# Two frequency classes per row in the intermediate matrix, and half of three constant matrices loaded instead of whole

## The chip, the cores and the metric

The kernel runs on one core of a Trainium2 chip. The metric is the time of one execution on the device in microseconds (us); lower is better. TensorE multiplies matrices from SBUF into the eight banks of PSUM; VectorE and ScalarE move results from PSUM to SBUF and do the elementwise work; GpSimd (POOL in the profile) clears tiles and issues DMAs; SyncE (SP) issues DMAs. All tiles have 128 partitions.

## What is computed

For `x` of 8 batches x 5696 positions x 128 channels and a filter `h` of 5696 x 128:

```
Xf = rfft(x, n=2*S, axis=1);  Hf = rfft(h, n=2*S, axis=0)
y  = irfft(Xf * Hf, n=2*S, axis=1)[:, :S, :]        # long convolution, per channel
X  = rfft(y, axis=1)                                # S = 5696
Y[:, :64] = X[:, :64] mixed by the complex 128x128 matrices w_r[m] + i*w_i[m]; the other modes are 0
u   = y + irfft(Y, n=S, axis=1)
out = u + relu(u @ w_ch)
```

Inputs and output are float32. The kernel computes in float16 with float32 sums.

## The kernel before, in words

**Names.** S = 5696 = 64 x 89 positions. J = 64, NQ = 89. The frequencies of the long transform fall into NK = 90 classes k of 64 each. The batches are worked on in four pairs (g_ = 0 to 3). NT = 23 ticks of four classes (the last has two) make up a pair's pass.

**Forward stages.** The first stage transforms over the 89 rows (`a_tile`, tile As), the second, per class, over the 64 (`tick`, tile M). In `products` the spectrum is multiplied by the filter's spectrum Hs into U, on VectorE. In two of three ticks ScalarE first casts the spectrum out of PSUM into Xs, and VectorE reads two SBUF tiles; in the others it reads PSUM.

**Z.** Two ticks later TensorE multiplies U by the constants Wc, and ScalarE casts the result into a buffer Zs or Zt: 128 rows (real and imaginary part of 64 positions p), and per class 256 numbers (two batches x 128 channels). SyncE stores each tick's Z to the DRAM scratch `zscr`, with a DMA row of 256 numbers (512 B) for each class and row. One tick later Z is also multiplied by the constants G. That sums the 64 low modes of y into PSUM bank 7, from which they go to XT.

**Mode products.** After the last pair 128 matmuls with 16 columns each multiply XT by the weights W (loaded during the last pair's ticks), giving Y. Eight transposes by the identity Id turn Y into C.

**Last stage.** `u_z` makes y from Z, `u_c` adds the 64 modes, and both sum in the same PSUM banks, four pairs of banks in turn (`LSLOT`). `u_tile` casts a half tile (eight positions p x 89, one batch) into UT, on ScalarE or VectorE by a fixed pattern whose first cast is VectorE's. `o_tile` multiplies UT by w_ch and the identity (tile WI), and ScalarE and VectorE make the output rows, which SyncE stores.
Z comes back in 16 chunks (four per pair, each 16 positions p of all classes). Row (k, real or imaginary) is the contracted index, 180 rows in all: the first 128 in the tile ZT`i`a with the constants S4a, and the other 52 in partitions 32 to 83 of ZT`i`b with the constants S4b (84 partitions used, of which the first 32 are cleared by GpSimd). So each position p takes two matmuls of 89 columns. The modes take one matmul with the constants IB (tile IBs) per four positions. S4a, S4b and IB have 5696 columns, in the order p, q.

**Five chunk buffers.** There are NC = 5 pairs of ZT tiles. They lie over space that the earlier stages have used: chunks 0 and 2 over Hs, 1 and 3 over As, 4 over M and G. `load_zt` (L469) issues the loads. Chunks 0 to 4 are issued by GpSimd, and per chunk in this order: first half, clear of 32 partitions (L477), second half. Chunks 5 to 15 are issued by SyncE as soon as the chunk five before has been used.

**What sets the order.** Each engine works through its own list in the order in which the program records it; a recorder adds semaphore waits from the named tokens of reads and writes. GpSimd's list in the last pair is written out in the dictionary `early` (L492), keyed by tick: Id and the four quarters of W, S4b at tick 12, S4a at tick 16, and at tick 21 chunk 0, IB, chunk 1 and chunk 2. Each also waits for the product of its tick (`pace`), and chunk 0 for the stores of Z up to tick 14 (`SLACK`). After the last tick come WI and chunks 3 and 4.
TensorE's list at the change of stage is: filler matmuls, the 128 mode products, `u_z` without the modes for the first two half tiles (`alone`, each bank opened by a matmul on a zeroed strip of F1), the eight transposes, `u_z` for a third half tile, and then the regular half tiles. The casts of Y (L304 on VectorE, L300 on ScalarE) and C (L306, L302) stand between them.
Lines of helpers in the profile: L300, L302 (ScalarE casts, without and with a scale), L304, L306 (the same on VectorE), L309 (every DMA), L312 (every matmul), L528 (the products), L690 (the transposes), L735 and L736 (the output's relu and sum).

Of the kernel before, what the change touches and what calls it, by code (L numbers as in the profile page):

```python
# [4 lines left out]
P = 128  # L5
# [118 lines left out]
def bass_long_conv_fft__then__afno_spectral_mix_kernel(nc, x, h, moe_w_r, moe_w_i, moe_w_ch, out):  # L124
# [3 lines left out]
    J = 64  # L128
# [29 lines left out]
    s4 = np.stack([back[:, None, None] * np.cos(ang), -back[:, None, None] * np.sin(ang)], axis=0)  # L158
    RB, PB = 2 * NK - P, 32
    rows = s4.transpose(1, 0, 2, 3).reshape(2 * NK, S)  # L160
    s4t = np.zeros((P, 2 * S))
    s4t[:, 0:S] = rows[0:P]
    s4t[PB:PB + RB, S:2 * S] = rows[P:2 * NK]
    tt = np.arange(S)
# [22 lines left out]
    c_s4 = const("cS4", s4t)  # L187
    c_ib = const("cIB", ib.reshape(P, -1))
    c_g = const("cG", g)
# [12 lines left out]
    def take(nbytes):  # L202
# [36 lines left out]
    f1_sb = at("F1", 2 * NK, F16, take(2 * NK * 2))  # L239
    wc_sb = at("Wc", 2 * P, F16, take(2 * P * 2))  # L240
    XTW = 3 * M
    xt = at("XT", B * XTW, F16, a_g + GW * 2 + 2048 * (NZX - NZ))
    assert GW * 2 + 2048 * (NZX - NZ) + B * XTW * 2 <= HW * 2

    ZB = 16
    NC = 5
    ZP = ZB * 2 * D
    a_h2, a_xt = a_h + HW * 2, a_x + 4 * S + 2 * B * P
    a_as1, a_m2 = a_as + 2 * S, a_m + 4 * S
    zt_off = [(a_h, a_h2), (a_as1, a_as1 + 2 * ZP), (a_h + 2 * ZP, a_h2 + 2 * ZP), (a_as1 + 4 * ZP, a_as1 + 6 * ZP),  # L250
              (a_m2, a_g)]
    assert 2 * S + 8 * ZP <= AW * 2
    zt = [[at(f"ZT{i}{'ab'[p_]}", ZP, F16, zt_off[i][p_]) for p_ in range(2)] for i in range(NC)]
    ib_sb = at("IBs", S, F16, a_m)
# [4 lines left out]
    u_sb = [at(f"UT{i}", S, F16, u_off[i]) for i in range(4)]  # L259
    o_big = [a_h + 4 * ZP, a_h2 + 4 * ZP, a_st + 4 * S] + [a_g + 2 * ZP + 4096 * i for i in range(2)] + \  # L260
            [a_xt + 4096 * i for i in range(2)]
# [22 lines left out]
    R = Recorder(nc)  # L284
    for name, n in (("c", 16), ("x", 26), ("z", 8), ("w", 16), ("t", 10), ("s", 8), ("o", 12), ("p", 16), ("q", 10)):
        R.ring(name, n)
# [87 lines left out]
    for i in range(MP):  # L374
        lo, hi = i * KP * 3 * J, (i + 1) * KP * 3 * J + (J if i == MP - 1 else 0)
        dma("gpsimd", m_sb[:, lo:hi], bass.AP(c_m, lo, [[MW, P], [1, hi - lo]]), "x", (), [("m", i)])
    dma("sync", wc_sb[:, :], bass.AP(c_w, 0, [[3 * P, P], [1, 2 * P]]), "c", (), [("wc",)])

# [87 lines left out]
    ZX = [("zs", i, b) for i in range(NZ, NZL) for b in range(2)]  # L466
    zt_old = [(H_ALL, H_ALL), (AST, AST), (H_ALL, H_ALL), (AST, AST), (M_ALL[3:6], G_ALL)]

    def load_zt(i, eng="sync", more=()):  # L469
        g_, c_ = divmod(i, J // ZB)  # L470
        for part, (p0, r0, n) in enumerate(((0, 0, P), (PB, P, RB))):
            old = once(("zt", i % NC, part), zt_old[i % NC][part])
            if more:
                old = list(old) + list(more)
            if old and part:
                z32 = zt[i][1][0:PB, :].bitcast(U32)
                R.add("gpsimd", lambda e: e.memset(z32, 0), (), [("zt0", i)], after=old)  # L477
            dma(eng, bass.AP(zt[i % NC][part], p0 * ZP, [[ZP, n], [1, ZP]]),
                bass.AP(zs, (g_ * 2 * NK + r0) * J * 256 + c_ * ZB * 256, [[J * 256, n], [1, ZP]]),
                "q" if eng == "gpsimd" else "t", [("zd", g_, s_) for s_ in range(NT)], [("zt", i % NC, part)], after=old)  # L480

    def load_ib():
        dma("gpsimd", ib_sb[:, :], c_ib.ap(), "p", (), [("ib",)], after=M_ALL[0:2] + pace)

    def load_s4(part):
        n = PB + RB if part else P
        dma("gpsimd", s4_sb[part][0:n, :], bass.AP(c_s4, part * S, [[2 * S, n], [1, S]]), "p", (),
            [("s4", part)], after=pace + (AST if part else M_ALL[1:4]))

# [3 lines left out]
             12: lambda: load_s4(1), 16: lambda: load_s4(0),  # L493
             NT - 2: lambda: (load_zt(0, "gpsimd", SLACK), load_ib(), load_zt(1, "gpsimd"), load_zt(2, "gpsimd"))}
    pace = []
# [41 lines left out]
    def tick(g_, t):  # L537
# [22 lines left out]
        if LC <= t < NT + LC:  # L560
            s_ = t - LC
            n = len(ticks[s_])
            i, zi = s_ % NU, s_ % NZS[g_]
            zb = [turns("z", ZBANK) for b in range(2)]
            for b in range(2):
                for r in range(2):
                    mm(pv(zb[b], 0, [[1, n * D]]), (W1, W2)[r], u_s[i][:, r * 1024 + b * 512:r * 1024 + b * 512 + n * D],
                       r == 0, r == 1, [("u", i), ("wc",)], [bank(zb[b])])
                evac(bass.AP(z_s[zi], b * D, [[1024, P], [2 * D, n], [1, D]]),
                     pv(zb[b], 0, [[D, n], [1, D]]), [bank(zb[b])], [("zs", zi, b)], eng="scalar",  # L570
                     after=once(("zx", zi, b), Z_OLD) if zi >= NZ else ())
            zo = (g_ * NK + KT * s_) * P * 256
            dma("sync", bass.AP(zs, zo, [[256, P], [P * 256, n], [1, 256]]),
                bass.AP(z_s[zi], 0, [[1024, P], [256, n], [1, 256]]), "z",
                [("zs", zi, 0), ("zs", zi, 1)], [("zd", g_, s_)])
# [45 lines left out]


    load_wi()
    load_zt(3, "gpsimd")
    load_zt(4, "gpsimd")

# [5 lines left out]
    def u_z(i, b, half, alone=False):  # L632
# [3 lines left out]
        for hb in range(2):  # L636
# [5 lines left out]
            for pl in range(4):  # L642
                for ri in range(2):
                    pz = half * 8 + hb * 4 + pl
                    so = (c_ * ZB + pz) * NQ
                    n = (P, PB + RB)[ri]
                    mm(pv(t + hb, pl * NQ, [[1, NQ]]), z[ri][0:n, pz * 256 + b * P:pz * 256 + b * P + P], s4_sb[ri][0:n, so:so + NQ],
                       False, not alone and pl == 3 and ri == 1, [("zt", i % NC, ri), ("zt0", i % NC), ("s4", ri)], [bank(t + hb)])
        if alone:
# [3 lines left out]
    def u_c(i, b, half, t, hb, first_):  # L653
# [3 lines left out]
           ib_sb[:, (c_ * ZB + pl0) * NQ:(c_ * ZB + pl0 + 4) * NQ], first_, not first_,  # L657
           [("c", g_ // 2), ("ib",)], [bank(t + hb)])

# [15 lines left out]

    XTT = [(n, g_) for g_ in range(NP) for n in ("xt", "xtn")]
    keep(10, 4)
    for m in range(M):
# [5 lines left out]
    for hb in range(2):  # L684
        evac(bass.AP(y_sb, hb * 32 * B, [[2 * M * B, P], [B, 32], [M * B, 2], [1, B]]),
             pv(hb, 0, [[2 * B, 32], [B, 2], [1, B]]), [bank(hb)], [("y", hb)], eng="scalar" if hb else "vector",
             after=ZY)
# [6 lines left out]
    for hb in range(2):  # L694
        evac(c_sb[:, hb * 512:hb * 512 + 512], ps16[:, (2 + hb) * 1024:(2 + hb) * 1024 + 512], [bank(2 + hb)],
             [("c", hb)], 2.0 * 64 / S, eng="vector" if hb else "scalar", after=WT)


    n_o = [0]
    o_cur = [0]  # L700
    o8_old = [H_ALL] * 2 + [U_ALL] + [G_ALL + ZX] * 2 + [WT] * 2
    o_old = [H_ALL] * 2 + [M_ALL[5:6]]
# [98 lines left out]
```

## Time and profile before

| what | us |
|---|---|
| three timed runs | 404.64, 406.85, 407.57 (median 406.85) |
| the profiled execution, its time | 409.74 |
| its span in the trace | 407.7 |
| TensorE busy | 376.7 (92%) |
| VectorE busy | 311.8 (76%) |
| ScalarE busy | 296.4 (73%) |
| GpSimd busy | 81.4 (20%) |

The DMA queues moved 105.81 MB in 86,720 packets, 72,286 of them under 2 KB. Queue q1 is SyncE's, q0 GpSimd's. In the profile a tile's buffer number is mostly left out, PE is TensorE, PEld its weight loads, DVE VectorE, ACT ScalarE. A line of the wait list reads: engine, tile, line, what it waited for, total us, times, longest. A line of the DMA issues reads: destination, source, queue, count, KB each, median us from issue to landing. Busy time of TensorE counts a matmul from its start to its modelled end, so its shares are read together with the clock.

### The profile page before, as it was taken

To read this page: it belongs to the slowest core of one execution; us is meant where nothing else is said; L and a number is where in the kernel's file an instruction comes from. 1 tells how busy PE (TensorE), PEld (TensorE's weight loads), DVE (VectorE), ACT (ScalarE), POOL (GpSimd) and SP (SyncE) were. 2 spreads that over 40 slices of the span, in tenths; PEclk is the share of its full clock that TensorE was granted. 3 is DMA by queue.
4 is the path that set the end of the run, shared out by engine and by line. 5 is a ranking of instruction groups with operands and counts; after the bars stand their busy time and mean duration, and the time that the engine had idled before them with its cause. 6 is when DMAs were issued, how large, how long until landed. Compare 5 with 4: busy or idle time off the path is not lost.

```text
span 407.7 us, 12527 instructions
## 1 busy us (share of the span) xinstructions
PE 376.7 (92%) x5398; PEld 286.7 (70%) x5398; DVE 311.8 (76%) x341; ACT 296.4 (73%) x477; POOL 81.4 (20%) x133
## 2 busy tenths in 40 slices
PE   7979899998999988899989899997978999999994
PEld 7978666656756657656658666665767889888873
DVE  6878789997899997889997888850324677777876
ACT  1458599987978977788878888960434777777775
POOL 8300022210823202723304011039100000000000
PEclk9999999999999999999999999995798999999999
DMA  8997379995989993989985499999998999999869
GB/s 159 194 320 271 101 162 280 274 278 159 138 137 218 251 233 80 141 154 207 245 224 95 48 311 346 285 274 394 417 390 340 314 350 420 406 419 390 347 251 357
DMA packets 86720, 105.81 MB, mean 260 GB/s; under 512 B 22494, under 2 KB 72286, under 8 KB 82846
## 3 DMA queue, kind: packets, MB, share of 16 engines
q1 hardware_dynamic: 62379, 67.73, 48.1%
q0 software_dynamic: 24288, 37.31, 43.0%
q8 instruction: 42, 0.69, 0.7%
q14 instruction: 11, 0.09, 0.1%
HBM read 72.49 MB, written 51.12 MB: 303 GB/s over the span
## 4 chain that ended last, share of the span: by engine, by line
PE 56%; DMA 14%; DVE 11%; ACT 9%; POOL 6%; issue 2%; SPq 0%; DVEq 0%; POOLq 0%
PE ps L312 56%; DVE U L528 5%; DMA ZT4b<-zscr 5%; DVE As L306 5%; DMA Xr<-in_x_dram 4%; ACT As L302 4%; DMA zscr<-Zt 3%; POOL Xr L309 2%; DMA Hs<-Hs 2%; ACT Xs L300 2%; ACT R L735 1%; ACT UT L300 1%; ACT Zt L300 1%; DVE Xin L348 1%; POOL ZT1b L477 0%
## 5 line engine op out<-in xcount | busy, mean ns | idle before, releaser
L528 DVE TENSOR_TENSOR U<-Xs,Hs 128x2048 f16<-128x2048 f16 x70 | 82.7, 1190 | 20.2 <-ACT Xs L300 20.0
L312 PE MATMUL ps<-U,Wc 128*128 128x512 f16 (+1 forms) x368 | 93.6, 377 | 1.9 <-DVE U L528 1.9
L300 ACT CAST Zs<-ps 128x512 f16<-128x512 f32 (+1 forms) x142 | 75.7, 592 | 9.4 <-PE ps L312 9.4
L300 ACT CAST Xs<-ps 128x1024 f16<-128x1024 f32 x70 | 69.4, 996 | 15.6 <-PE ps L312 14.6
L736 DVE TENSOR_TENSOR O<-ps,R 128x512 f32<-128x512 f32 x81 | 52.5, 685 | 20.4 <-ACT R L735 12.0
L735 ACT ACTIVATE R<-ps 128x512 f32<-128x512 f32 x96 | 50.9, 572 | 18.8 <-PE ps L312 18.4
L306 DVE TENSOR_SCALAR As<-ps 128x720 f16<-128x720 f32 x68 | 57.6, 900 | 9.1 <-PE ps L312 8.5
L312 PE MATMUL ps<-As,M 64*128 64x128 f16 x1440 | 55.8, 217 | 5.1 <-ACT Xs L300 2.0
L312 PE MATMUL ps<-F,Xin 128*128 128x180 f16 x512 | 53.5, 249 | 7.0 <-DVE As L306 2.8
L312 PEld LDWEIGHTS ps<-F,Xin 128*128 128x128 f16 x512 | 44.6, 155 | 14.5 <-DVE As L306 4.1
L302 ACT ACTIVATE As<-ps 128x720 f16<-128x720 f32 x60 | 46.3, 785 | 10.6 <-PE ps L312 9.7
L312 PE MATMUL ps<-WI,UT 128*128 128x256 f16 x360 | 52.3, 280 | 0.5 <-DVE O L736 0.4
L312 PEld LDWEIGHTS ps<-As,M 64*128 64x128 f16 x1440 | 40.7, 94 | 15.1 <-DVE U L528 3.2
L312 PEld LDWEIGHTS ps<-U,Wc 128*128 128x128 f16 x368 | 29.1, 98 | 31.6 <-DVE U L528 2.4
L528 DVE TENSOR_TENSOR U<-ps,Hs 128x2048 f16<-128x2048 f32 x22 | 50.2, 2283 | 0.8 <-DMA Hs<-Hs 0.8
L309 POOL DMA_DIRECT2D Xt<-in_x_dram x48 | 25.5, 536 | 109.7 <-PE ps L312 94.7
L300 ACT CAST UT<-ps 128x712 f16<-128x712 f32 x40 | 30.0, 752 | 20.7 <-PE ps L312 19.7
L312 PEld LDWEIGHTS ps<-WI,UT 128*128 128x128 f16 x360 | 39.4, 152 | 4.3 <-issue 1.9
L312 PE MATMUL ps<-IBs,C 128*128 128x356 f16 x128 | 40.6, 327 | 0.6
L312 PEld LDWEIGHTS ps<-G,Zs 128*128 128x128 f16 x556 | 28.1, 96 | 14.9
L304 DVE CAST UT<-ps 128x712 f16<-128x712 f32 x24 | 21.4, 891 | 17.0 <-PE ps L312 17.0
L312 PE MATMUL ps<-G,Zs 128*128 128x128 f16 (+2 forms) x556 | 34.3, 192 | 0.0
(84 smaller groups left out, 497.0 us busy)
## 6 DMA issues: line engine op xcount, KB each, us to landing
out_dram<-O SPq DMA_DIRECT2D x39, 512.0 KB, 8.3
zscr<-Zs SPq DMA_DIRECT2D x68, 256.0 KB, 6.2
Xt<-in_x_dram POOLq DMA_DIRECT2D x24, 320.0 KB, 6.9
zscr<-Zt SPq DMA_DIRECT2D x20, 256.0 KB, 6.9
W<-wscr POOLq DMA_DIRECT2D x4, 1024.0 KB, 8.5
M<-cM POOLq DMA_DIRECT2D x5, 720.0 KB, 20.4
ZT0a<-zscr SPq DMA_DIRECT2D x3, 1024.0 KB, 9.9
Hs<-Hs SPq DMA_DIRECT2D x44, 64.0 KB, 5.9
```

The lines of the kernel that those rows point to most:

```text
L300: R.add(e, lambda h_: h_.copy(dst, src), reads, writes, after=after)
L302: R.add(e, lambda h_: h_.activation(dst, src, COPY, scale=scale), reads, writes, after=after)
L304: R.add(e, lambda h_: h_.tensor_copy(dst, src), reads, writes, after=after)
L306: R.add(e, lambda h_: h_.tensor_scalar_mul(dst, src, scale), reads, writes, after=after)
L309: R.add(eng, lambda h_: h_.dma_start(dst, src), reads, writes, ring=ring, after=after)
L312: R.add("tensor", lambda h_: h_.matmul(o, l, r, start=st, stop=sp), reads, writes)
L348: R.add("vector", lambda e: e.tensor_copy(bass.AP(x_sb, i * XN * XS, [[XW, NQ], [XS, XN], [1, D]]), bass.AP(src, 0, [[XB, NQ], [D, XN], [1 ...
L528: R.add("vector", lambda e: e.tensor_tensor(uv, src, hv, MULT), bk + [("h", t, 0), ("h", t, 1, 0), ("h", t, 1, J)], [("u", i)])
L735: R.add("scalar", lambda e: e.activation(rv, src_r, RELU), bk, [("r", i % NR)], after=once(("r", i % NR), G_ALL + XTT + [("y", 0), ("y", 1 ...
L736: R.add("vector", lambda e: e.tensor_tensor(ov, src_u, rv, ADD), bk + [("r", i % NR)], [key + (h_,)], after=once(key, old))
```

## The change

**Z by pairs of classes.** `zscr` now holds, per pair of classes (k, k+1) and row p, 512 numbers side by side. A store writes rows of 512 numbers (1 KB), half as many. A chunk's contracted index becomes (pair of classes, real or imaginary), 90 rows of 16 positions x 512 numbers (16 KB). The two matmuls of a position p take the even and the odd class of the same rows.

**Rows spread.** A chunk is one tile ZT`i` of 128 partitions. 64 rows go to partitions 0, 2, ..., 126 and 26 rows to partitions 1, 5, ..., 101. The other 38 partitions must be zero, so GpSimd clears the whole tile (128 x 4096 words of 4 bytes) once, before its first load. The clears of chunks 1 and 0 are recorded at ticks 14 and 17, those of 2, 3 and 4 just before their loads. All chunk loads, 5 to 15 too, are issued by GpSimd.

**Half of the constants.** S4a and S4b (now the constants of the even and the odd classes) and IB are loaded only for the positions p = 0 to 32 (SH = 33 x 89 = 2937 columns). S4a and S4b are cleared by GpSimd first (128 x 2848 words each) and loaded in the same spread rows. The columns of p = 33 to 63 are those of 64 - p, read backwards, with a sign that depends on the row: `reflect` multiplies by a column of the small table SG (128 x 3, loaded by SyncE). VectorE makes the mirrored part of S4a and IB, ScalarE that of S4b. Those of S4 are recorded before the mode products, that of IB after the casts of C. The chunks with p from 32 on wait for them.

**Moved with it.** The two casts of Y change engines (the first bank's to ScalarE, the second's to VectorE). Two of the output buffers move from the space of G to that of M. GpSimd's ring of chunk semaphores grows from 10 to 12.

```diff
+    SH = (J // 2 + 1) * NQ
+    s4t = s4[..., :].transpose(1, 0, 2, 3).reshape(NK // 2, 2, 2, S).transpose(0, 2, 1, 3)[..., 0:SH].reshape(NK, 2 * SH)
+    sg = np.ones((P, 3))
...
-    c_ib = const("cIB", ib.reshape(P, -1))
+    c_ib = const("cIB", ib.reshape(P, -1)[:, 0:SH])
...
+    SPREAD = ((0, J, 0, 2), (J, NK - J, 1, 4))
...
+    zt = [at(f"ZT{i}", 2 * ZP, F16, zt_off[i]) for i in range(NC)]
...
+    zt_old = [H_ALL, AST, H_ALL, AST, G_ALL + ZX + ZY]
+
+    def load_zt(i, more=()):
         g_, c_ = divmod(i, J // ZB)
+        old = list(once(("zt", i % NC), zt_old[i % NC])) + list(more)
+        for part, (r0, n, p0, st) in enumerate(SPREAD):
+            dma("gpsimd", bass.AP(zt[i % NC], p0 * 2 * ZP, [[st * 2 * ZP, n], [1, 2 * ZP]]),
+                bass.AP(zs, g_ * NK * P * 256 + r0 * J * 512 + c_ * ZB * 512, [[J * 512, n], [1, 2 * ZP]]),
+                "q", [("zd", g_, s_) for s_ in range(NT)] + [("zc", i % NC)], [("zt", i % NC, part)], after=old)
+
+    def clear_zt(i):
+        z32 = zt[i][:, :].bitcast(U32)
+        R.add("gpsimd", lambda e: e.memset(z32, 0), (), [("zc", i)], after=list(zt_old[i]) + pace)
...
+    def reflect(eng, t, n, col, key, after):
+        MN = S - SH
+        dst, src = bass.AP(t, SH, [[S, n], [1, MN]]), bass.AP(t, SH - NQ - 1, [[S, n], [-1, MN]])
+        sc = sg_sb[0:n, col:col + 1]
...
+            R.add(eng, lambda e: e.activation(dst, src, COPY, scale=sc), toks, [key + (1,)], after=after)
...
+            R.add(eng, lambda e: e.tensor_scalar_mul(dst, src, sc), toks, [key + (1,)], after=after)
...
+        s32 = s4_sb[part][:, :].bitcast(U32)
+        R.add("gpsimd", lambda e: e.memset(s32, 0), (), [("s4z", part)], after=old)
+        for h_, (r0, n, p0, st) in enumerate(SPREAD):
+            dma("gpsimd", bass.AP(s4_sb[part], p0 * S, [[st * S, n], [1, SH]]), bass.AP(c_s4, (r0 * 2 + part) * SH, [[2 * SH, n], [1, SH]]),
+                "p", [("s4z", part)], [("s4", part, 0, h_)], after=old)
...
              12: lambda: load_s4(1), 16: lambda: load_s4(0),
-             NT - 2: lambda: (load_zt(0, "gpsimd", SLACK), load_ib(), load_zt(1, "gpsimd"), load_zt(2, "gpsimd"))}
+             14: lambda: clear_zt(1),
+             17: lambda: clear_zt(0),
+             NT - 2: lambda: (load_zt(0, SLACK), load_ib(), load_zt(1), clear_zt(2), load_zt(2))}
...
-            dma("sync", bass.AP(zs, zo, [[256, P], [P * 256, n], [1, 256]]),
-                bass.AP(z_s[zi], 0, [[1024, P], [256, n], [1, 256]]), "z",
+            dma("sync", bass.AP(zs, zo, [[512, P], [P * 512, n // 2], [1, 512]]),
+                bass.AP(z_s[zi], 0, [[1024, P], [512, n // 2], [1, 512]]), "z",
...
+    pace[:] = []
     load_wi()
-    load_zt(3, "gpsimd")
-    load_zt(4, "gpsimd")
+    clear_zt(3)
+    load_zt(3)
+    clear_zt(4)
+    load_zt(4)
...
+    reflect("vector", s4_sb[0], P, 0, ("s4", 0), M_ALL[1:4])
+    reflect("scalar", s4_sb[1], P, 1, ("s4", 1), AST)
     keep(10, 4)
...
+    reflect("vector", ib_sb, P, 2, ("ib",), M_ALL[0:2])
```

## The prediction

> **What bounds the kernel now.** I read the page's forty slices first, then the wait list, the chain of waits, the DMA issues, and two-microsecond windows around the gap. The slices:
>
> ```profile
> DVE  6878789997899997889997888850324677777876
> PEclk9999999999999999999999999995798999999999
> DMA  8997379995989993989985499999998999999869
> ```
>
> A slice is 10.2 us. Up to 270 us, and again from 312 us, TensorE is nearly always busy (its share is 99% in the stretch 320 to 340). Between them, in slices 27 to 31, VectorE falls to 0 to 5 tenths, the granted TensorE clock falls to 5 tenths, and only the DMA stays full. The windows there (columns: TensorE, weight loads, VectorE, ScalarE and GpSimd busy time, then granted clock, DMA share, GB/s):
>
> ```profile
> 276.00:278.00 2.00, 1.85 (x51) 1.44 (x47) 0.29 (x1) 0.52 (x1) 2.00 (x3) 0.52 0.91 295
> 278.00:280.00 2.00, 0.23 (x1) 0.10 (x1) 0.00 (x0) 0.07 (x1) 2.00 (x3) 0.50 1.14 409
> 288.00:290.00 2.00, 2.00 (x13) 1.09 (x11) 0.90 (x1) 0.78 (x2) 0.00 (x0) 0.56 1.03 420
> 304.00:306.00 2.00, 0.20 (x1) 0.10 (x1) 0.00 (x0) 0.29 (x1) 0.00 (x0) 1.00 0.99 389
> 308.00:310.00 2.00, 2.00 (x20) 1.65 (x18) 0.90 (x1) 0.56 (x1) 0.00 (x0) 0.50 0.81 336
> ```
>
> TensorE stands still twice, at 278 to 280.8 and 303.6 to 307, and it works at half clock from about 276 to 289.6 and from 306.9 to 310.2. The wait list between 270 and 320 us names the causes:
>
> ```profile
> POOL ZT0a L309 <- DMA zscr<-Zt: 10.0, 1, 10.0
> PE ps L312 <- DMA ZT4b<-zscr: 2.4, 1, 2.4
> PE ps L312 <- DMA ZT0b<-zscr: 2.4, 1, 2.4
> PE ps L312 <- DMA ZT3b<-zscr: 0.7, 1, 0.7
> PE ps L312 <- DMA ZT4a<-zscr: 0.7, 1, 0.7
> ```
>
> All are loads of the Z chunks. The chain of waits says why they are late:
>
> ```profile
> 260.02 10.88 DMA zscr<-Zt
> ...
> 271.95 1.81 POOL ZT0b L477
> 273.76 0.46 POOL ZT0b L309
> ...
> 286.47 20.44 DMA ZT4b<-zscr
> ```
>
> The first Z load waits until a Z store issued at 260.0 has landed at 270.9; then GpSimd clears 32 partitions (1.8 us) between the two halves of each chunk; and the last half of chunk 4, issued at 286.5, needs 20.4 us. Transfers of the same kind took, by the DMA issues (KB each, us to landing):
>
> ```profile
> ZT1a<-zscr POOLq DMA_DIRECT2D x1, 1024.0 KB, 12.0
> S4b<-cS POOLq DMA_DIRECT2D x1, 934.5 KB, 8.5
> ZT0b<-zscr POOLq DMA_DIRECT2D x1, 416.0 KB, 7.1
> ZT4b<-zscr POOLq DMA_DIRECT2D x1, 416.0 KB, 20.4
> ```
>
> The 20.4 us are a queue: from 290.8 on, SyncE issues chunks 5 to 8 (5.9 MB) on its own queue, and they share the DMA with chunks 3 and 4 that GpSimd issued before.
>
> **The change, part by part.** The profiled execution took 409.74 us (span 407.7, 2.0 around it), which is 2.9 above the median 406.85 of the three runs and above all of them. I sum against 409.74 and carry the difference to the median.
>
> *Z stores.* The 46,080 rows of 512 B (4 pairs x 90 classes x 128) become 23,040 of 1 KB. Most transfers of Z are written while TensorE is busy, so this shows only as relief of the DMA. Windows rich in 512 B rows move 268 to 271 GB/s at shares of 0.86 to 0.96 (264 to 268 us); windows of 8 KB reads move 409 to 446. A store of 256 KB therefore costs at most 0.97 us of DMA and at least 0.6; I take 0.77 for the 1 KB rows, between them. Over the last pair's 11 ticks from 250 to 270 us that is 2.2 us of DMA time. Before 250 us the only stalls on transfers are VectorE's, on Hs (0.8 us) and on Xt (1.1 us): gain 0 to 1.9, taken 0.5.
>
> *Constants.* S4a, S4b and IB shrink from 3782 KB to 1767 KB (2 x 90 rows and 128 rows of 5874 B). At 410 GB/s that is 5.0 us of DMA time, 3.3 of them before 270 us. Together with the stores, some 5 us of backlog vanish before 270, so the store that the first load waits for should land near 265. The next gate is the pacing on the last product but one, which VectorE ends at 269.9. So the first Z load starts about 270.0 instead of 271.4.
>
> *GpSimd's new order.* A memset of 32x2048 words took 1.82 us, 0.89 ns a word; 128 partitions should cost no more, as the four 128x1 memsets at the start took 0.10 to 0.11 us each. So a chunk's clear (4096 words) costs 3.65 us and S4's (2848) 2.53. Two of each come before the first load, with four issues of 0.53: from 253.5 (S4b's start in the trace) the chain is S4b to 257.1, chunk 1 to 260.8 (its product, of tick 14, ends at 257.0), S4a from its present gate at 260.9 to 264.5, chunk 0 to 268.1. That leaves 1.8 us until 269.9: no cost, but thin. Then chunk 0 is issued by 271.0 (its second half left at 273.7 before), IB by 271.6, chunk 1 by 272.7, the clear and issues of chunk 2 by 277.4, WI, chunk 3 by 283.2, chunk 4 by 287.9, against 287.0 before. Chunk 4 gets 0.9 us later and is not needed until about 300.
>
> *Chunk 0.* Its landing takes between 3.4 us (1440 KB at 420 GB/s) and 12.0 (chunk 1's row); nearest is ZT0b's own 7.1, with less traffic ahead of it. From 270.6 that gives 277.7. TensorE ends the mode products and the filler matmul at 277.85 and restarted at 280.84: 3.0 us of standstill go. That work is at half clock. If the clock comes back at 289.6 as now, the 3.0 us are worth 1.5; if it comes back one dip (3.3 us, the length of the second one) sooner, 1.65 more; two sooner, 3.3 more. Range 1.5 to 4.8, taken 3.0.
>
> *Chunks 3 and 4.* All loads are now on GpSimd's queue, so chunk 5 comes behind chunk 4. A chunk is 1440 KB, 3.6 us of DMA at 410 GB/s, and TensorE takes 3.93 us for one (SyncE's chunk loads left at 290.80, 294.73, 298.67). Chunk 4 lands by 288 + 7.1 = 295, and is needed at 300. The waits of 0.7, 0.7 and 2.4 us go (3.8), and with them the second dip, 3.3 us at half clock: 1.65. Lower end: half, if the queue is still late (below); upper end 5.45.
>
> *Reflections.* ScalarE's on S4b: 2759 elements at the 996 ns per 1024 of the Xs casts, 2.7 us. VectorE's: between 0.92 us (the Xin copy, 2048 in 0.68) and 3.07 (2048 in 2.28 from PSUM); I take 3.07, as the start is odd and the source runs backwards. The two on S4 run from 273.4 to 276.5. Queued behind them are the Y casts (ready at 275.6 and 277.5) and behind those the transposes, which TensorE reaches at about 282: hidden; if that cover were gone, 3.1 us. IB's waits on VectorE for the C cast, about 283.2, and ends at 286.3. Behind it stands the first UT cast, ready at 285.6, whose bank TensorE wants back two half tiles later. Price 0 to 3.1, taken 0.6.
>
> *Nothing else on the path.* Matmuls keep their number and their 89 columns; 84 rows become 128, and both kinds took 203 ns medians. SyncE loses 22 issues in the last stage (0.3 to 0.9 us each) and GpSimd, idle there, gains them. The later stage needs a chunk every 6.7 us, far slower than they load. The small sign table loads at the start, ahead of Wc, which is not needed before 30 us.
>
> Sum: 0.5 + 3.0 + 3.8 + 1.65 - 0.6 = 8.35 us. 409.74 becomes 401.4, and on the median's scale 406.85 becomes **398.5**. Its own range, from the ends above, is 394.5 to 402.5.
>
> **Rivals.**
>
> *The reflection waits for GpSimd.* IB's reflection and the clear of chunk 4 (283.2 to 286.8) want to start together. If the clear goes first and holds VectorE, the reflection ends at 289.9, the first UT cast at 290.8, and TensorE loses up to 3.6 us less the half tile it has in hand: 401. Against it: the Y cast of 0.69 us ran at 275.6 inside a GpSimd memset at its normal length (O's 685 ns for as many elements); but that read PSUM, and no row has VectorE reading and writing SBUF beside a memset. [...]
>
> *The transfers stay late.* The DMA share is 0.8 to 1.14 in every window from 276 to 310, so a new order makes no bandwidth. If chunk 0 gains nothing and chunk 4 only the 1.7 us of the smaller IB, the second dip stays, and some 2.3 us with the 0.5 above remain: 404.5. Against it: chunks 5 to 8, which competed with 3 and 4, move behind them.
>
> *Slower: the clears under the products.* From 250 to 270 us VectorE is busy for 16.76 of 20 us, and GpSimd has no memset there now. If a clear advances only while VectorE rests (16% of the time), 2.7 of the 12.4 us are done by 269.9; the other 9.7 and the 2.1 of issues put the first load at 281.7 and its landing at 289.3, 8.5 later than now. With 5.45 still won behind it, 0.6 paid and the rest lost to the longer idle clock: 411. It decides from about 1.6 ns a word on: then chunk 0 lands 5 us late and the change is worth nothing. For it: only 1.8 us of slack. Against it: 0.89 ns in all five memsets, but all with VectorE idle or on PSUM.
>
> **How the numbers follow.** Forecast 0.56 (394.5 to 402.5); reflection held 0.08 (401); transfers late 0.20 (404.5); slower 0.16 (411). About 1%, 4.1 us, is what a measurement can tell from no change: below 402.8 is faster, above 410.9 slower. Faster: 0.56 + 0.07 + 0.03 = 0.66. Same: 0.01 + 0.17 + 0.03 = 0.21. Slower: 0.13. The range 394.5 to 405.0 leaves out the slower rival and the tails.
>
> **What would show it.** Right: memsets of 128x4096 at 3.6 us and none ending after 270; chunk 0 issued near 270; no wait of TensorE on any ZT load; no second clock dip; the reflections at 0.9 to 3.1 us with the first UT cast no later than 288. Wrong: a ZT4 wait of microseconds (transfers), memsets over 5 us before 270 (slower), or a reflection that begins just as a memset ends (held). What would make the number wrong with the mechanism right is mainly where the clock returns.

## The result, and the profile after

The changed kernel takes 424.27 us (median of four runs, 421.12 to 424.42), the kernel before in the same comparison 406.26. The ratio is 1.043, with a 95% interval from 1.036 to 1.049: slower by 4.3%, where 398.5 was forecast. Medians here and below are over all runs of a kernel, while ratios leave out its slow runs (over 1.5% above its fastest), one of which, of e15_place, took 855.43 us for a reason that nothing here shows. The profiled execution took 424.37 us, with a span of 422.6.

The forty slices of the changed kernel, now 10.6 us each, show where the time went:

```profile
PE   7989899989899989899998999989699539989995
PEclk9999999999999999999999999968999888989999
DMA  7996399994989949999937897898899989997669
```

Counted from 0, slices 26 and 27 are the change of stage: the clock falls to 6 and 8 tenths, where before it fell to 5, 7 and, once more, 8. The loss stands later, in slices 31 and 32 (327 to 349 us), with TensorE at 5 and 3 tenths and a clock of 8. The DMA is at 8 to 9 tenths there, as full as around it. The windows (columns as in the prediction) place it:

```profile
270.00:290.00 20.00, 18.58 (x279) 13.96 (x278) 8.10 (x8) 7.81 (x13) 12.85 (x13) 0.74 0.98 316
312.00:330.00 18.00, 17.87 (x262) 15.94 (x261) 13.81 (x22) 13.12 (x24) 2.92 (x6) 1.00 1.01 384
330.00:350.00 20.00, 8.82 (x85) 6.72 (x84) 4.64 (x9) 5.25 (x9) 1.05 (x2) 0.80 0.92 348
```

From 330 to 350 us TensorE works 8.82 of 20 us (19.81 before). The wait list from 270 us on names what it waits for (six of its lines):

```profile
POOL ZT L484 <- PE ps L316: 9.4, 1, 9.4
DVE Os L761 <- DMA out_dram<-Os: 8.6, 1, 8.6
PE ps L316 <- DVE Os L761: 6.8, 1, 6.8
PE ps L316 <- DMA ZT<-zscr: 4.9, 3, 3.0
DVE O L761 <- DMA out_dram<-O: 4.8, 1, 4.8
PE ps L316 <- DVE O L761: 4.8, 2, 4.4
```

Read from below: TensorE waits for VectorE's output sums (L761), because VectorE waits for output buffers, whose stores have not landed. The chain of waits has one such store, and the late load of chunk 4 ahead of it:

```profile
270.07 0.53 POOL ZT L313
270.60 8.34 DMA ZT<-zscr
278.94 0.05 issue
...
292.94 3.52 POOL ZT L484
...
297.45 6.66 DMA ZT<-zscr
304.11 0.05 issue
304.16 13.92 PE ps L316 x183
...
320.17 26.43 DMA out_dram<-Os
```

Chunk 0 is issued at 270.07, and TensorE goes on at 279.0 (280.8 before). The clear of chunk 4 starts only at 292.94. At 304.16 the changed kernel is still 2.8 us ahead of this execution of the one before (306.95; e18 below shows another). Then a store of output rows needs 26.4 us to land; the longest before took 12.9.

The trace also holds every DMA packet. A chunk row of 8192 bytes took 309 ns before, and 92% of the rows were within a tenth of that. A row of 16,384 bytes takes 611 ns at best, the same rate (26.8 bytes a ns against 26.5), but only 58% were within a tenth of it, and the mean is 742. In stretches of 4 us in which chunk rows filled the DMA engines (97% of their busy time), the loads moved 403 GB/s before and 329 after.

### The profile page after: what moved, and what is told of

Same layout as the page of the kernel before. It is cut to its first block, busy times and chain, and to the rows that moved or that the text cites. A ratio compares the mean times of both kernels' runs of the same rounds, so it can differ in the third digit from the quotient of the medians.

```text
span 422.6 us, 12550 instructions
## 1 busy us (share of the span) xinstructions
PE 381.1 (90%) x5398; PEld 288.7 (68%) x5398; DVE 316.5 (75%) x343; ACT 299.4 (71%) x478; POOL 107.6 (25%) x159
## 4 chain that ended last, share of the span: by engine, by line
PE 55%; DMA 17%; DVE 13%; ACT 6%; issue 4%; POOL 3%; SPq 0%; DVEq 0%; POOLq 0%
PE ps L316 55%; DVE U L547 7%; DMA out_dram<-Os 6%; DVE As L310 4%; DMA Xr<-in_x_dram 4%; DMA ZT<-zscr 4%; ACT As L306 2%; ACT Xs L304 2%; POOL Xr L313 2%; DMA Xt<-in_x_dram 2%; DMA Hs<-Hs 2%; POOL ZT L484 1%; ACT UT L304 1%; ACT R L760 1%; DVE Xin L352 1%
## 5 line engine op out<-in xcount | busy, mean ns | idle before, releaser
L761 DVE TENSOR_TENSOR O<-ps,R 128x512 f32<-128x512 f32 x81 | 52.7, 685 | 27.2 <-ACT R L760 16.7
L316 PE MATMUL ps<-S4a,ZT 128*128 128x89 f16 x512 | 61.3, 212 | 6.6 <-DMA ZT<-zscr 4.9
L316 PE MATMUL ps<-WI,UT 128*128 128x256 f16 x360 | 55.2, 291 | 11.7 <-DVE Os L761 6.8
L316 PE MATMUL ps<-S4b,ZT 128*128 128x89 f16 x512 | 61.5, 213 | 0.0
L316 PEld LDWEIGHTS ps<-S4a,ZT 128*128 128x128 f16 x512 | 48.6, 103 | 8.2 <-DMA ZT<-zscr 5.8
L316 PEld LDWEIGHTS ps<-S4b,ZT 128*128 128x128 f16 x512 | 47.2, 103 | 8.7 <-issue 1.8
L316 PEld LDWEIGHTS ps<-WI,UT 128*128 128x128 f16 x360 | 40.4, 154 | 16.8 <-issue 13.7
## 6 DMA issues: line engine op xcount, KB each, us to landing
M<-cM POOLq DMA_DIRECT2D x5, 720.0 KB, 20.7
```

Of the source, the lines that this page charges most:

```text
L316: R.add("tensor", lambda h_: h_.matmul(o, l, r, start=st, stop=sp), reads, writes)
L761: R.add("vector", lambda e: e.tensor_tensor(ov, src_u, rv, ADD), bk + [("r", i % NR)], [key + (h_,)], after=once(key, old))
```

## The experiments

Three theories at first. A: two queues; the loads, now on GpSimd's queue, take the DMA from the stores on SyncE's. B: the load rows themselves are slow. C: the late chunk 4 bunches the loads. From the fifth run on the question was why the rows are slow: B1 the spread, B2 the size of the row, B3 the partitions that the rows land on. For the runs that bear on the rows, the chunk rows from 272 us on (the rate is that of the 4-us stretches above; e4 ran once, e5, e9, e11, e13 and e14 twice, as did e10 below; each ratio is to runs of the kernel before in the same comparison):

| run | rows land on | mean ns of a row | within 10% of the best | GB/s | median us | ratio to before |
|---|---|---|---|---|---|---|
| before | 128: all; 52: 32 to 83 | 335 (8 KB) | 92% | 403 | 406.3 | |
| after | 64: 0, 2, ...; 26: 1, 5, ... | 742 | 58% | 329 | 424.3 | 1.043 |
| e4_flat | the same | 758 | 55% | 310 | 429.6 | |
| e6_half | the same | 369 (8 KB) | 60% | 291 | 418.8 | 1.028 |
| e5_unspread | 0 to 89 | 1039 | 3% | 214 | 455.7 | 1.118 |
| e9_port | 64: 32 to 95; 26: 96 to 121 | 815 | 58% | 289 | 438.4 | 1.076 |
| e11_only64 | 64: 32 to 95 | 705 | 80% | 419 | 400.3 | 0.982 |
| e13_64_every2nd | 64: 0, 2, ..., 126 | 734 | 75% | 402 | 401.1 | 0.985 |
| e14_64_first | 64: 0 to 63 | 1080 | 3% | 208 | 427.4 | 1.049 |
| e15_place | 64: 0, 2, ...; 26: 33, 35, ..., 83 | 657 | 87% | 407 | 412.6 | 1.016 |
| e17_place_sync_zs6 | the same | 646 | 94% | 403 | 403.5 | 0.994 |
| e8_gpq | as before | 327 (8 KB) | 96% | 391 | 410.4 | 1.008 |

**e1_sync.** Chunks 5 to 15 go back to SyncE's queue.

```diff
-            dma("gpsimd", bass.AP(zt[i % NC], ...
-                "q", ...
+            dma("gpsimd" if i < NC else "sync", bass.AP(zt[i % NC], ...
+                "q" if i < NC else "t", ...
```

> The changed kernel, but chunks 5 to 15 are issued by SyncE again. Theory A (sharing): the loss is made by the queue. GpSimd's 16 KB rows alternate row by row with the 4 KB rows of the output stores, the stores starve (26 us to land) and TensorE waits for output buffers from 331 to 347 us. Then, in one queue, loads and stores take turns by transfer: no store over 13 us, no wait of the output sums for a store, and about 405 us, as the changed kernel was 2.8 us ahead of the one before at 304 us. Theory B (slow loads): the 16 KB rows need 640 to 860 ns where two 8 KB rows needed 618, so a chunk costs 4.4 us of DMA instead of 3.5, whoever issues it; the DMA then falls short by about 0.9 us for each of 11 chunks, TensorE waits for chunks or buffers elsewhere, and the time stays at 412 to 420. Theory C (chunk 4): the clear of chunk 4 waits for the last Z store until 292.9 us, and chunks 4 to 8 are issued in one bunch; with SyncE issuing 5 to 8 the bunch is gone, so C too expects about 405, but it expects the same from the kernel in which only that wait is removed.

Measured: 423.5 us, ratio 1.038 (1.030 to 1.046), no faster than the change within the interval. The wait list of this run:

```profile
PE ps L316 <- DMA ZT<-zscr: 13.8, 4, 9.1
```

No output buffer is waited for over 3.1 us in all; TensorE waits for chunks instead, 13.8 us. In the change, with two queues, rows of both kinds start in every 2 us from 314 to 344 us (23 to 42 of 16,384 bytes, 34 to 64 of 4096). On one queue the wait only moves from the stores to the loads, and the time stays (423.5 us against 424.3). So A alone falls. The rows were slower still than in the change, 825 ns on average against 742, and 803 in the next run; no run says why.

**e2_zs6.** The last pair uses six buffers of Z again, so the clear of chunk 4 has no store from a Zt buffer to wait for.

```diff
-    NZS = [NZ] + [NZX] * (NP - 2) + [8]
+    NZS = [NZ] + [NZX] * (NP - 2) + [NZ]
...
-    SLACK = [("zd", NP - 1, s_) for s_ in range(NT - NZL)]
+    SLACK = [("zd", NP - 1, s_) for s_ in range(NT - 8)]
```

> The changed kernel, but the last pair uses only the six Zs buffers for Z, so that the clear of chunk 4 no longer waits for a late Z store (the gate of the first load is kept at the same tick). Theory C: chunk 4's clear starts at about 283.5 instead of 292.9, chunk 4 is there before TensorE needs it (3 us of wait and a clock dip less), loads 5 to 8 are not bunched, the stores do not starve: 403 to 408. Theory A: the wait for chunk 4 goes (3 to 5 us), but the loads still run ahead on their own queue and the stores still starve: 416 to 420, with the wait for output stores still in the trace. Theory B: as A.

Measured: 426.98 us, 1.047 (1.040 to 1.055). The waits for output buffers stay:

```profile
DVE Os L761 <- DMA out_dram<-Os: 10.5, 1, 10.5
DVE O L761 <- DMA out_dram<-O: 7.4, 2, 4.9
```

C falls as the main cause.

**e3_both.** Both edits.

> Both edits: chunks 5 to 15 by SyncE, and the last pair's Z in six buffers. Theory A: the two losses are separate, so this is e1 less 3 to 5 us: 400 to 402. Theory B: no better than e1 by more than 1 us, since the slow loads bind; 411 or more. Theory C: the same as e1 and e2 within 2 us.

Measured: 424.03 us, 1.038 (1.030 to 1.047). Both together do not help either while the rows are slow.

**e4_flat.** The rows are read one behind the other from DRAM, without the step of 64 KB; Z's numbers are then in the wrong places.

```diff
-  ... g_ * NK * P * 256 + r0 * J * 512 + c_ * ZB * 512, [[J * 512, n], [1, 2 * ZP]]
+  ... g_ * NK * P * 256 + (c_ * NK + r0) * 2 * ZP, [[2 * ZP, n], [1, 2 * ZP]]
```

> The changed kernel, but each chunk load reads its 90 rows of 16 KB one behind the other in DRAM instead of 64 KB apart, so the chunks hold the wrong numbers; sizes, partitions and queues are unchanged. It tells where the slow rows of 640 to 860 ns come from. If the DRAM side (the 64 KB pitch) is the cause, the rows fall to about 618 ns and a chunk alone on the DMA moves at 410 to 420 GB/s instead of 330. If the SBUF side (the spread partitions) is the cause, they stay at 770 to 800 ns where nothing else is moved.

Measured: 429.56 us in one run, and rows as slow as in the change (table). The step in DRAM is not it.

**e5_unspread.** All 90 rows on neighbouring partitions. Here and in the runs below that change SPREAD, the rows of S4 move too, and the sign table with them (not shown in the diffs).

```diff
-    SPREAD = ((0, J, 0, 2), (J, NK - J, 1, 4))
+    SPREAD = ((0, J, 0, 1), (J, NK - J, J, 1))
```

> The changed kernel with the 90 rows of S4 and of each chunk on 90 neighbouring partitions (0 to 89) instead of spread over every second and every fourth partition; nothing else differs. Theory B1 (the wide spread itself makes the 16,384-byte rows take 640 to 1000 ns where an undisturbed one takes 611): rows at 611 ns, pure loading at 1.6 MB per 4 us or more, and about 407 to 412 us. Theory B2 (the row's size makes them slow, wherever the rows land): rows stay at 650 to 1100 ns, and 420 to 428 us. [...]

Measured: 455.69 us, 1.118 (1.107 to 1.129), hardly a row at 611 ns (3% within a tenth, 1039 on average), 214 GB/s. For B3 I had estimated rows above 1000 ns and over 430 us. So B3 holds: the partitions decide, and 0 to 89 are worse; why, no trace shows. B1 falls.

**e6_half.** Two transfers with rows of 8192 bytes for each part (with a longer ring of semaphores, not shown).

```diff
+            for v_ in range(2):
+                dma("gpsimd", bass.AP(zt[i % NC], p0 * 2 * ZP + v_ * ZP, [[st * 2 * ZP, n], [1, ZP]]), ...
```

> The changed kernel with each chunk load issued as two transfers per part, each with rows of 8192 bytes (8 positions) instead of one with 16,384; layout, order and engines as in the changed kernel, and the matmuls wait for the whole chunk as before. Theory B2 (the size of the row is what costs): rows of 8192 bytes take 309 ns as in the kernel before, pure loading moves 1.65 MB per 4 us, the output stores get their share back, and 405 to 412 us. Theory B1 (the spread costs, whatever the size): rows of 8192 bytes take 330 to 500 ns and the time stays at 418 to 426.

Measured: 418.84 us, 1.028 (1.021 to 1.035). The rows did not become faster: 60% near 309 ns, 291 GB/s. B2 falls as the reason of the rate. The 5.4 us won are not explained by any run here; the same two transfers on SyncE's queue (e10_half_sync) gave nothing more:

> The changed kernel with rows of 8192 bytes (as in the run that gave 418.8) and chunks 5 to 15 issued by SyncE (one queue with the output stores). With the slow rows left in place (half of them over 350 ns), a chunk still costs some 4.5 to 5 us. If queue sharing adds its own loss on top (the kernel before lost 2.6 to 4 us by it), 413 to 417; if the slow rows alone decide, 417 to 421, with waits of TensorE for ZT in place of those for output buffers.

Measured: 417.75 us, 1.025 (1.018 to 1.031), in the range of its second case; TensorE waits for ZT in place of output buffers (11.2 us in all). The slow rows decide.

**e7_mirror.** The kernel before, with one part of the change alone: half of S4 and IB loaded, the other half mirrored, in the old rows.

```diff
+    s4t = np.zeros((P, 2 * SH))
+    s4t[:, 0:SH] = rows[0:P, 0:SH]
+    s4t[PB:PB + RB, SH:2 * SH] = rows[P:2 * NK, 0:SH]
...
+    reflect("vector", s4_sb[0], P, 0, ("s4", 0), M_ALL[1:4])
+    reflect("scalar", s4_sb[1], PB + RB, 1, ("s4", 1), AST)
...
+    reflect("vector", ib_sb, P, 2, ("ib",), M_ALL[0:2])
```

> The kernel before with one part of the change alone: half of S4 and half of IB loaded and the other half made by VectorE and ScalarE; Z stays in the old layout of 180 rows of 8192 bytes. All theories of the loss put it in the chunk loads, so this should not lose: between 401 (about 1.4 MB less to move ahead of 280 us at about 400 GB/s is 3.5 us less for the loads of chunks 0 to 4, of which a little shows) and 407 (hidden). Over 411 would say that the mirrored half itself costs.

Measured: 405.45 us, 0.993 (0.989 to 0.997). This part is good by 0.7%, small but clear of 1 by its interval.

**e8_gpq.** The kernel before, with chunks 5 to 15 issued by GpSimd (and its ring of semaphores longer, not shown).

```diff
-    def load_zt(i, eng="sync", more=()):
+    def load_zt(i, eng="gpsimd", more=()):
```

> The kernel before with chunks 5 to 15 issued by GpSimd, so that loads and output stores come from two queues, as in the changed kernel, but with rows of 8192 bytes. Theory A (a load queue beside a store queue starves the stores, whatever the rows): output stores of 4096-byte rows land in over 20 us, VectorE waits for its output buffers, and 412 to 424 us. Theory B (slow 16,384-byte rows are needed for it): 404 to 410 us, with no wait for an output buffer over 2 us.

Measured: 410.42 us, 1.008 (1.004 to 1.012). Two queues cost the kernel before some 3 us with rows at full speed (96% within a tenth of 309 ns), and its wait list has the same kind of line as the change, only smaller:

```profile
DVE Os L736 <- DMA out_dram<-Os: 4.7, 3, 2.3
```

So A is true, as a small part of the loss.

**e9_port.** The 64 rows on 32 to 95, the 26 on 96 to 121.

```diff
-    SPREAD = ((0, J, 0, 2), (J, NK - J, 1, 4))
+    SPREAD = ((0, J, 32, 1), (J, NK - J, 96, 1))
```

> The changed kernel with the 64 rows of a part on partitions 32 to 95 and the 26 rows on 96 to 121, all neighbouring; nothing else differs. [...] Rival (neighbouring rows are slow as such): all rows at about 1200 ns, and over 440 us.

Measured: 438.44 us, 1.076 (1.067 to 1.084): worse than the 412 to 424 of my own estimate, which had the 64 rows at the 611 ns of the change's best and the 26 near the 1200 of e5 (1183 ns is the mean of its 90 rows from 272 to 290 us), and just under the rival's 440, though the mean row of 815 ns is far from its 1200. There is one heap (56% of the rows from 600 to 650 ns) and a flat tail from 650 to 1500, with no second heap at 1200. The trace does not name the partition of a row. This run could not tell the two parts of a load apart, and the next three left the 26 rows out.

**e11_only64, e13_64_every2nd, e14_64_first.** Only the first 64 rows, on 32 to 95, on the even partitions as in the change, and on 0 to 63. The line below is common to the three; e11 has the SPREAD of e9, e13 that of the change, e14 that of e5. All three move the same bytes in the same rows, and the other 26 rows of Z count as zero.

```diff
-        for part, (r0, n, p0, st) in enumerate(SPREAD):
+        for part, (r0, n, p0, st) in enumerate(SPREAD[0:1]):
```

> The kernel of the run with rows on partitions 32 to 95, with the second part of each chunk load (26 of 90 rows) left out, so those rows of Z count as zero. [...] If rows of this size are slow by themselves when loads and stores mix, a good part stays above 800 ns.

> The changed kernel with the second part of each chunk load left out (26 of 90 rows of Z count as zero) and the first 64 rows where the change puts them, on partitions 0, 2, ..., 126. It moves the same bytes in the same rows as the run with 64 rows on partitions 32 to 95, which loaded at 419 GB/s and took 400.3 us. Theory B3 (where the rows land): the only difference is the partitions, and the rows are slower: 300 to 380 GB/s in pure loading, fewer than 70% of the rows near 611 ns. Rival (in the changed kernel only the 26 rows on every fourth partition are slow, or they slow the others): about 419 GB/s and 80% near 611 ns, as there. The time in both cases between 399 and 408, as 29% of the load is gone.

> As the run before, with the 64 rows on partitions 0 to 63. Theory B3: nearly all rows near 1200 ns and 205 to 220 GB/s, as in the run with all 90 rows on 0 to 89, so that even 71% of the load is slower than the whole load in the kernel before: 415 to 440 us. Rival (neighbouring rows are slow only with the second part beside them): 611 ns and over 400 GB/s, about 400 us.

Measured, in this order: 419, 402 and 208 GB/s; 400.3, 401.1 and 427.4 us. The landing place alone makes a factor of two. On the even partitions the 64 rows are nearly as fast as on 32 to 95, so my expectation for e13 failed and its rival held: in the change it is the 26 rows on every fourth partition that are slow, or that slow the others. With 71% of the load, 0 to 63 is slower (427.4 us) than the whole load of the kernel before (406.3). Why 0 to 63 is slow and 32 to 95 is not, no trace shows.

**e15_place.** Only the second part of 26 rows moves, to 33, 35, ..., 83, the range in which the kernel before lands its second part.

```diff
-    SPREAD = ((0, J, 0, 2), (J, NK - J, 1, 4))
+    SPREAD = ((0, J, 0, 2), (J, NK - J, 33, 2))
```

> The changed kernel with the second part's 26 rows on partitions 33, 35, ..., 83 instead of 1, 5, ..., 101; nothing else differs. The 64 rows on even partitions loaded at 402 GB/s without the second part, and the whole load at 329 with it, so what is slow is the second part. The rows on partitions 32 to 95 loaded at 419 GB/s and the kernel before lands its 52 rows on 32 to 83. [...]

Measured: 412.60 us, 1.016 (1.012 to 1.020): 11.7 us less than the change, from moving 26 rows. The rate is 407 GB/s. I had estimated 385 to 420 GB/s and 399 to 408 us if the place of the 26 rows is what costs, near the 402 of e13 and the 419 of e11, and 300 to 340 GB/s and 418 to 426 us if any second part slows the 64 rows. The rate is in the first range, the time 4.6 us above it. So the place is what cost. Why this place is better than 1, 5, ..., 101 is not shown: both the range and the step changed, and no run changed one alone, and the trace names neither the partition nor the engine of a packet. What is left of the waits is A:

```profile
DVE Os L761 <- DMA out_dram<-Os: 8.5, 1, 8.5
PE ps L316 <- DVE Os L761: 7.7, 1, 7.7
```

**e16_place_sync, e17_place_sync_zs6.** With the edit of e1 as well, and then with that of e2 too.

> The kernel of the run before with chunks 5 to 15 issued by SyncE, on one queue with the output stores, as in the kernel before. If two queues cost as much here as they did the kernel before (2.6 to 3.9 us), 397 to 404; if full-speed rows make the queue's order unimportant, the same as the run before within 1.5 us.

> Both edits and the last pair's Z buffers back to six, so that the clear of chunk 4 has no store of Zt to wait for (it waited until 292.9 us in the changed kernel). If that wait costs what TensorE stood still for chunk 4 (3.0 us and a clock dip of 3.4 us at half speed), 2 to 4 us under the run before; if it is covered once the loads are fast, the same. My forecast of the change, 398.5 on the scale of the median of before, should be met here if its terms other than the loads' speed were right: 396 to 402.

Measured, on the same chip as e15: 409.48 us, 1.010 (1.006 to 1.013), and 403.48 us, 0.994 (0.990 to 0.997). With one queue the wait for output buffers is gone, and the next in line shows, chunk 4:

```profile
PE ps L316 <- DMA ZT<-zscr: 6.0, 1, 6.0
POOL ZT L484 <- PE ps L316: 5.4, 1, 5.4
```

Without the late clear (e17) no wait of TensorE after 262 us is over 0.6 us:

```profile
PE ps L316 <- DVE UT L308: 0.6, 1, 0.6
PE ps L316 <- DVE O L761: 0.4, 1, 0.4
PE ps L316 <- DMA ZT<-zscr: 0.4, 1, 0.4
```

The same two edits that gave nothing in e1 to e3 give 9.1 us once the rows are fast. They were true losses behind a larger one. The 6.0 of chunk 4 is clear of noise; the 3.1 of the queue is less sure, as the intervals of e15 and e16 overlap.

**e12_mirror_clear.** e7 with the clears of chunks 0 to 2 moved under the products, in the old rows.

```diff
+             14: lambda: clear_ztb(1), 17: lambda: (clear_ztb(0), clear_ztb(2)),
```

> The kernel before with two parts of the change: the mirrored halves of S4 and IB, and the clears of chunks 0 to 2 moved ahead (32 partitions by 4096 elements each, 1.8 us each, under the products of the last pair instead of between the issues). Z stays in the old layout. Theory: the clears leave GpSimd's chain ahead of chunk 0, which is then issued 1.8 us earlier, and chunks 1 and 2 up to 5 us earlier; with the halves alone TensorE still waited 2.9 us for chunk 0, so 403 to 405 us. Rival (the DMA engines are full from 270 to 290 us, share 0.94, so an earlier issue lands no earlier): the same as with the halves alone, 405.5.

Measured: 402.92 us, 0.988 (0.983 to 0.992), at the lower end of what its theory gave. The chain of e12 shows the issues without clears between them:

```profile
271.53 0.53 POOL ZT0a L316
272.06 0.53 POOL ZT0b L316
272.58 0.53 POOL IBs L316
```

With e7 and e17 it is one of three complete versions that beat both kernels. The intervals of e12 and e17 overlap, so nothing here shows a gain of the new rows of Z over the old ones. The mirrored halves are what is shown to be worth keeping; the early clears probably are: TensorE's wait for chunk 0, 2.9 us in e7, is not in e12's profile, but the intervals of e7 and e12 overlap too.

**e18_before_again.** The kernel before, unchanged, for a second profile.

> The kernel before, unchanged, to see a second profiled execution. The prediction's sum was made against one execution of 409.74 us, 2.9 above the median, and its terms for chunks 3 and 4 (waits of 0.7, 0.7 and 2.4 us, and 1.65 for the clock dip behind them) come from it. If those waits belong to the kernel, a run near 406 shows them too, with a dip near 307 us. If they are what made that execution long, this one has less than 2 us of them and perhaps no second dip, and then 3 to 5 us of the forecast gain were never there in the median.

Measured: this execution took 405.34 us (409.74 was the first one). Its wait list for TensorE between 262 and 420 us is short:

```profile
PE ps L312 <- DMA ZT0b<-zscr: 2.7, 1, 2.7
PE ps L312 <- DVE O L736: 0.4, 1, 0.4
```

and its clock falls once:

```profile
PEclk9998999999999999999999999998599999999999
```

The waits for chunks 3 and 4 and the second dip are not there. TensorE begins chunk 4 at 303.6 us here, so the lead that the changed kernel had at 304.16 over the first profile is no lead over this one.

## Why the prediction was wrong

It was wrong by 25.8 us, and on the wrong side. The runs divide this as follows: 11.7 for the place of the 26 rows (e15), 3.1 for the queue (e16), 6.0 for chunk 4 (e17), and 5.45 for two terms that the second profile of before does not hold (e18). That makes 26.2. The division belongs to this order of edits: taken alone, the queue and chunk 4 gave nothing.

- **"A chunk is 1440 KB, 3.6 us of DMA at 410 GB/s": failed.** The rate was that of the old rows. At 329 GB/s a chunk costs 4.5 us. The change put the rows on other partitions, and I gave that no price and no rival, though "rows spread" was one of its parts. No row of the trace of before shows it. This is the largest loss: 11.7 us by e15, which moves only the 26 rows of a chunk and those of S4.
- **"SyncE loses 22 issues ... and GpSimd, idle there, gains them", at nothing: failed.** With the loads and the output stores on two queues VectorE waited 8.5 us for the landing of one store (e15); with both on one queue no such wait is left in its list (e16). 3.1 us by e16; 3 us in the kernel before by e8.
- **"Chunk 4 by 287.9": failed.** Its new tile lies over the Zt buffers of the last stores, so its clear had to wait for them: the last was issued at 272.1 and landed 20.7 us later, at 292.8, just ahead of the clear (the wait list above names TensorE for this wait). I listed what the clears follow on GpSimd, but not which buffer each one overwrites. In e17 the same clear ended at 287.6 and the load left at 287.9, near what I had (286.8 and 287.9). 6.0 us, once the rows are fast.
- **The terms of 3.8 and 1.65 for chunks 3 and 4: mis-sized.** They were real in the profile of before, an execution of 409.74 us, and absent in the second one of 405.34; two profiles do not say how often they occur. Waits of one execution that lies above the median should not have been counted as a gain of the median.
- **Chunk 0, 3.0 us: about right.** Issued at 270.07 (270.0 forecast), landed 1.2 us later than the 277.7 of the forecast; in e16, with the rows fast, TensorE restarted at 277.6. The clock stayed at half for 10.24 us (13.65 in both profiles of before), one dip sooner. What then remains of the sum is 0.5 + 3.0 - 0.6 = 2.9 us, and e17 is 2.8 below the kernel before. That they agree so closely is partly luck: the 0.5 can hardly be seen (VectorE's two stalls on Hs and Xt, 1.9 us in all, were 1.5 in the change and 1.7 in e18).
- **Clears under the products (the slower rival): refuted.** They run at the forecast price beside a busy VectorE (3.51 and 3.54 us for 128x4096, 3.51 to 3.55 for the three later ones) and end at 267.8 (268.1 forecast):

```profile
252.93 2.47 POOL L502 MEMSET S4b<- 128x2848 uint32 x1 [6.28 <-PE ps L316]
257.03 3.51 POOL L484 MEMSET ZT<- 128x4096 uint32 x1 [0.26 <-PE ps L316]
264.29 3.54 POOL L484 MEMSET ZT<- 128x4096 uint32 x1
```

- **The reflections: hidden, as forecast, but one was held.** VectorE's part of the timeline:

```profile
273.20 3.75 DVE L497 TENSOR_SCALAR S4a<-S4a,SG 128x2759 f16<-128x2759 f16 x1
284.37 0.93 DVE L497 TENSOR_SCALAR IBs<-IBs,SG 128x2759 f16<-128x2759 f16 x1
286.86 0.90 DVE L308 CAST UT<-ps 128x712 f16<-128x712 f32 x1 [1.56 <-PE ps L316]
```

The same operation takes 0.93 us alone and 3.75 when it starts inside a clear on GpSimd (272.69 to 276.22); it ends 0.73 us after the clear. So the hold that the rival had is there. It met S4a, where the Y cast behind it had time until 277.4, and not IB, as chunk 4's clear was late. In e17, where that clear came early (284.03 to 287.56), it met IB as the rival said:

```profile
283.60 4.70 DVE L497 TENSOR_SCALAR IBs<-IBs,SG 128x2759 f16<-128x2759 f16 x1
288.22 1.69 DVE L308 CAST UT<-ps 128x712 f16<-128x712 f32 x2
```

IB's multiply took 4.70 us, and the first UT cast began at 288.22 (285.49 in e16, whose stage ran 0.6 us ahead). TensorE waited 0.6 us for that cast, its longest wait left in e17; the rival's 401 stands 2.5 above the forecast. So the 0.6 that I took came out right by luck, through a meeting that I had given a chance of 0.08. The multiply's record begins there 0.43 us before the clear's, and it still ended 0.74 after it; why it was held although it began first is not shown.
- **The transfers stay late (404.5): nearest in place, wrong in size.** It let the DMA keep its rate and only the order fail.
- **The range: tighter than its own terms.** Its slow end of 402.5 comes out only with the reflections at nothing. With their upper price of 3.1 us the low ends (0, 1.5 and 2.7) give 405.7.

## What to carry to other kernels

When a change moves the partitions on which a DMA lands, that is a new transfer (here 208 to 419 GB/s for the same 64 rows): bound its rate from both sides, even if bytes and row size look better. If waits stand in line, undoing one behind a larger one shows nothing; repeat the test once the first is gone. And take a gain only from waits that the median execution has: with one profile, look at how far it lies above the median before counting all of its stalls.

## What the runs showed of the hardware

- 64 rows of 16,384 bytes landed at 419 GB/s on partitions 32 to 95 (e11), at 402 on 0, 2, ..., 126 (e13), and at 208 on 0 to 63 (e14). Beside 64 rows on 0, 2, ..., 126, a second part of 26 rows brought the rate of the whole down to 329 on 1, 5, ..., 101 (the change) and left it at 407 on 33, 35, ..., 83 (e15).
- Rows of twice the length did not halve the DMA time of the Z stores: by medians a row of 512 B took 27 ns (before) and one of 1 KB 46 ns (the change), so 23,040 of the one take 15% less than 46,080 of the other.
- VectorE's multiply of 128x2759 between SBUF tiles took 3.75 us (the change) and 4.70 (e17) beside a GpSimd clear, against 0.93 alone. VectorE's products and the clears did not slow each other: from 250 to 270 us the products of 128x2048 took 1.23 us on average with two SBUF inputs and 2.28 with PSUM, both without clears (before) and beside four of them (the change), VectorE was busy for 16.76 of 20 us in both, and the clears of 128x4096 kept their length (3.51 and 3.54 us, against 3.51 to 3.55 later).
